# Attention and a SoLU feed-forward by two-level Strassen products: one operand made on GpSimd, and the last tile's steps moved to later slots

## The chip, the cores and the metric

The kernel runs on one NeuronCore of a Trainium2 chip. The metric is the device time of one launch in microseconds. Engines are named as in the profile: PE (TensorE; PEld is its weight load), DVE (VectorE), ACT (ScalarE), POOL (GpSimd), SP (the engine that issues most DMAs).

## The reference

```python
# q, k, v: (8, 12, 448, 64); g_q, g_k: (64,)
q_n, k_n = rmsnorm(q, g_q), rmsnorm(k, g_k)
attn = softmax(q_n @ k_n.T / sqrt(64))
x = (attn @ v).transpose(0, 2, 1, 3).reshape(3584, 768)
h = x @ w_in                              # w_in: 768 x 1024
e = exp(h - max(h)); solu = h * e / (sum(e) + 1e-9)
ln = (solu - mean(solu)) / sqrt(var(solu) + 1e-6) * g_ln
out = ln @ w_out                          # w_out: 1024 x 768
```

The change lies where the rows of `ln` are finished and the product with `w_out` begins.

## The kernel before

**Stages.** The first stage computes the attention and writes x to DRAM. The middle stage takes the 3584 rows as 28 tiles of 128 rows, in 14 groups g of two tiles (2g and 2g+1), and forms h = x w_in with Strassen's seven products (P1 to P7) per group. The last stage takes the normalized tiles four at a time, as 7 blocks n (block n has tiles 4n to 4n+3), and multiplies them by w_out with Strassen's scheme at two levels: seven outer products per block, each of seven inner products. The order of everything is written out by hand: each engine runs its instructions in the order in which the Python emits them, and the framework adds the semaphores.

**A tile's steps after its h is complete.** `ff_max` (DVE, tiny), `ff_exp` (ACT, L1067: u = exp(h - max)), `ff_mult` (DVE, L1071: u = h * u, which frees h), `ff_moments` (DVE: two batch-norm statistics L1079, their join L1080, three tiny instructions to L1084; then POOL: a power, L1085, called "pow" below, and "shift", L1087), `ff_norm` (ACT, L1091: u = u * e + shift), `ff_spread` (DVE: a transpose in blocks, L1100, from u to a buffer ub; then four stores on SP's queue, L1103, to the DRAM array ud of that tile). Multiplication, moments, scaling and spread in the title are `ff_mult`, `ff_moments`, `ff_norm` and `ff_spread`. Buffers h and u have three slots each and ub two, and the last stage's outputs use these same buffers in turn.

**When these steps are emitted.** `done(g, i)` is called inside products P4 (i = 1, tile 2g+1) and P3 (i = 0, tile 2g), the last two products of a group. It puts the five steps on a list with `later(x, f)`: due x units after the current one. A unit of the middle stage counts four steps, a slot of the last stage one. So for the last group (g = 13), a step of tile 27 given x is emitted in slot 4x - 9 of the last stage, a step of tile 26 (the tile that ends last) in slot 4x - 5; if that slot holds no product, in the next that does.

**Slots of the last stage.** One inner product is one slot: four matmul records of 128x192, KC = 2 chunks of two passes each. Outer product q (in the order P1, P5, P6, P2, P7, P3, P4 for each block; q counts on through the blocks) puts its seven inner products p1, p2, p6, p5, p7, p4, p3 into slots 7q + (0, 4, 8, 10, 12, 16, 20). So up to three outer products are interleaved, and from slot 14 on every slot is taken; slots 1, 2, 3, 5, 6, 9 and 13 are empty. Slot 20 is p3 of q = 0, slot 24 p5 of q = 2, slot 26 p7 of q = 2, slot 37 p4 of q = 3, slot 40 p7 of q = 4.

Three kinds of PSUM banks are used, A, B and C; B and C have two each (by q % 2), A four. p1 begins bank A and p6, p7, p4 go on adding to it, each after the one before has been read; p5 begins bank B and p3 adds to it; p2 uses C. What empties them:

- p1, p6, p7: the running sums q1, u2, u3 (L1222 on ACT for P1 and P5, else L1224 on DVE), and p4 likewise its result;
- p2: L1249 on DVE; p7 also reads bank B by L1262 on DVE; p3 by L1272 on DVE. So p5 of product q + 2 can begin only when L1272 of product q has read the same bank.

**Operands.** An outer product needs an operand of [128, 2, 4, 4, 32] (two token tiles, t = 0 and 1), made from the rows of ud that `load_u` brings back (L1147, SP) by `make(n, name, t)`, one instruction per t: a11, a12 and a22 are copies on ACT; s1, s2, s3, s4 are sums or differences on DVE (L1171, L1173, L1175, L1177). For block 0, a11 and s1 are made during the middle stage. From an operand `inner_sums` makes the four sums of the inner level with four POOL instructions of 128x256, L1188 to L1191, into one of four buffers. p1 and p2 (the halves of t = 0) and p4 (t = 1) use the operand itself, p6 the second of these sums, p5 the first, p7 the third, p3 the fourth.

`when(slot, f)` emits f at the end of a slot, after the product and after the steps due there. For block 0: s2 in slots 0 and 3, s3 in 6 and 8, a12 in 10 and 11, a22 in 12 and 14, s4 in 17 and 20; the sums of the operand of outer product q in slot 7q - 6, so those of s2 (q = 2) in slot 8, a12 15, s3 22, s4 29, a22 36. In slots 10 to 22 SP gets eight loads for block 1; in slots 18 and 21 ACT makes block 1's a11 and in slots 27 and 30 DVE its s1. V (L1300, DVE) is made in slots 31 and 34.

Of the kernel before, what the change touches and what calls it, by code (L numbers as in the profile page):

```python
# [14 lines left out]
OP = AluOpType  # L15
# [351 lines left out]
def fast_path(  # L367
# [24 lines left out]
    nc = tc.nc  # L392
# [11 lines left out]
    NG = NT // 2  # L404
# [535 lines left out]
    def load_x(g):  # L940
        x = gs[g, "x"] = xs.tile([P, KD, 2 * P], FP32, tag="x", name="xg")
        t = 2 * g * P
        while t < 2 * (g + 1) * P:
            b, c = divmod(t, S)
            n = min(S - c, 2 * (g + 1) * P - t)
            o = t - 2 * g * P

            (nc.sync if g < 2 else nc.scalar).dma_start(x[:, :, o : o + n], xd[b].rearrange("(c p) t -> p c t", p=P)[:, :, c : c + n])
            t += n

    def sizes(g):

        x = gs[g, "x"].rearrange("p c t -> p (c t)")
        n = HD * 2 * P
        sm = gs[g, "s"] = xs.tile([P, 3, HD, P], FP32, tag="x", name="xsum")
        for i in range(2):
            nc.scalar.activation(
                sm.rearrange("p k c t -> p (k c t)")[:, 0:n], x[:, i * n : (i + 1) * n], AF.Square,
                accum_out=xmax[:, 2 * g + i : 2 * g + i + 1],
            )  # L960
# [7 lines left out]
    def block_sums(g, part):  # L968

        if part == 0:  # L970
            gs[g, "A"] = x_blocks(g)
        a11, a12, a21, a22 = gs[g, "A"]
        sm = gs[g, "s"]
        s1, s2, s4 = [sm[:, i] for i in range(3)]
        if part == 0:
            nc.gpsimd.tensor_tensor(s1, a21, a22, OP.add)
            nc.gpsimd.tensor_tensor(s2, s1, a11, OP.subtract)
        else:
            nc.gpsimd.tensor_tensor(a21, a11, a21, OP.subtract)
            nc.gpsimd.tensor_tensor(s4, a12, s2, OP.subtract)  # L980
# [77 lines left out]
    def ff_max(t):  # L1058
        d = mt[t]
        d["nmax"] = small.tile([P, 1], FP32, tag="hmax", name="hmax")  # L1060
        nc.vector.tensor_scalar(d["nmax"], d["top"], -1.0, None, OP.mult)  # L1061
# [46 lines left out]
    def in_parts():  # L1108
        def done(g, i):
            t = 2 * g + i  # L1110
            ff_max(t)
            waits = {
                (NG - 2, 1): (1, 2, 3, 5, 5), (NG - 1, 1): (1, 2, 3.25, 6.75, 7), (NG - 1, 0): (2.25, 3.75, 4.75, 7.5, 8)
            }.get((g, i), (1, 2, 3, 5, 7))
            for x, f in zip(waits, (ff_exp, ff_mult, ff_moments, ff_norm, ff_spread)):
                later(x, lambda f=f: f(t))

        p = [products(g, lambda i, g=g: done(g, i)) for g in range(NG)]
        parts = [p[0][1], p[0][2]]
        for g in range(NG):  # L1120
            turn = [p[g][6], p[g][5], p[g][7], p[g][4], p[g][3]]
            x = len(parts)
            if g + 1 < NG:
                turn[3:] = [p[g + 1][1], p[g][4], p[g + 1][2], p[g][3]]
            parts += turn
            if g + 1 < NG:
                follow(parts, x, lambda g=g: sizes(g + 1))
                follow(parts, x + 1, lambda g=g: block_sums(g + 1, 0))
                follow(parts, x + 2, lambda g=g: block_sums(g + 1, 1))
            if g + 2 < NG:  # L1130
                follow(parts, x + 4, lambda g=g: load_x(g + 2))
        return parts

    ORDER = ("P1", "P5", "P6", "P2", "P7", "P3", "P4")
    STEP = 7
# [6 lines left out]
    us = {}  # L1142

    def load_u(n, t, h):
        own = last.get("u", last["first"])
        r = us[n, "raw", t, h] = own.tile([P, P * HF], FP32, tag="raw", name="ur", bufs=2 if own is last["first"] else 6)
        nc.sync.dma_start(r, ud[4 * n + t][h].rearrange("g j x -> (g j) x"))  # L1147

    def in_turn(n, t, h):
        return us[n, "raw", t, h].rearrange("p (a c i) -> p c a i", a=4, c=HF)  # L1150

    def operand(n, name):
        own = last.get("u", last["first"])
        if (n, name) not in us:
            us[n, name] = own.tile(
                [P, 2, HF, 4, 32], FP32, tag="op", name=name, bufs=2 if own is last["first"] else 8
            )
        return us[n, name]

    def make(n, name, t):  # L1160


        o = operand(n, name)[:, t]
        if name == "a11":
            nc.scalar.copy(o, in_turn(n, t, 0))
        elif name == "a12":
            nc.scalar.copy(o, in_turn(n, t, 1))
        elif name == "a22":
            nc.scalar.copy(o, in_turn(n, 2 + t, 1))
        elif name == "s1":  # L1170
            nc.vector.tensor_tensor(o, in_turn(n, 2 + t, 0), in_turn(n, 2 + t, 1), OP.add)  # L1171
        elif name == "s2":
            nc.vector.tensor_tensor(o, us[n, "s1"][:, t], us[n, "a11"][:, t], OP.subtract)  # L1173
        elif name == "s3":
            nc.vector.tensor_tensor(o, us[n, "a11"][:, t], in_turn(n, 2 + t, 0), OP.subtract)  # L1175
        else:
            nc.vector.tensor_tensor(o, us[n, "a12"][:, t], us[n, "s2"][:, t], OP.subtract)  # L1177

    def inner_sums(n, name):

        own = last.get("u", last["first"])
        a = us[n, name]
        sm = us[n, name, "sums"] = own.tile(
            [P, 4, KC, 4, 32], FP32, tag="sums", name="sums", bufs=2 if own is last["first"] else 4
        )
        a11, a12, a21, a22 = [a[:, t, k * KC : (k + 1) * KC] for t in range(2) for k in range(2)]
        s1, s2, s3, s4 = [sm[:, i] for i in range(4)]
        nc.gpsimd.tensor_tensor(s1, a21, a22, OP.add)  # L1188
        nc.gpsimd.tensor_tensor(s2, s1, a11, OP.subtract)
        nc.gpsimd.tensor_tensor(s3, a11, a21, OP.subtract)  # L1190
        nc.gpsimd.tensor_tensor(s4, a12, s2, OP.subtract)  # L1191
# [104 lines left out]
    def both(n, x, t):  # L1296

        if (n, x) not in us:
            us[n, x] = out_tile(x)
        nc.vector.tensor_tensor(us[n, x][:, t], us[n, "U2" if x == "V" else "U3"][:, t], us[n, "P5"][:, t], OP.add)  # L1300
        if x == "C22" and t == 0:
            store_y(n, us[n, x], 1, 1)

    def follow(p, i, f):
        g = p[i]

        def both():
            g()
            later(1, f)

        p[i] = both
# [7 lines left out]
    def later(units, f):  # L1319
        todo.append((now + 4 * units, f))  # L1320
# [49 lines left out]
    with tc.manual_schedule():  # L1370
# [228 lines left out]
        def when(slot, f):  # L1599
            at.setdefault(slot, []).append(f)  # L1600

        def made(n, name, *slots_of):
            for t, slot in enumerate(slots_of):
                when(slot, lambda t=t: make(n, name, t))

        period = STEP * len(ORDER)
        for n in range(NS):
            base = period * n
            for i, name in enumerate(ORDER):
                q = len(ORDER) * n + i  # L1610
                for place, f in zip(PLACES, outer_product(n, name, q)):
                    assert STEP * q + place not in slots
                    slots[STEP * q + place] = f
                x = HALVES[name][0]
                if q > 1:
                    when(STEP * q - 6, lambda n=n, x=x: inner_sums(n, x))
            for x, t, slot in (("V", 1, 31), ("V", 0, 34), ("C22", 1, 45), ("C22", 0, 52)):
                when(base + slot, lambda n=n, x=x, t=t: both(n, x, t))
            if n == 0:
                continue  # L1620
            base -= period
            at_load = (10, 11, 15, 16, 17, 18, 21, 22) if n == 1 else (4, 5, 8, 9, 10, 11, 16, 17)
            blocks = (0, 0), (1, 0), (2, 0), (3, 0), (2, 1), (3, 1), (0, 1), (1, 1)
            for slot, (t, h) in zip(at_load, blocks):
                when(base + slot, lambda n=n, t=t, h=h: load_u(n, t, h))
            late = 6 if n == 1 else 0
            made(n, "a11", base + 12 + late, base + 15 + late)
            made(n, "s1", base + 21 + late, base + 24 + late)
            made(n, "s2", base + 28 + late, base + 38)
            made(n, "a12", base + 33, base + 36)  # L1630
            made(n, "s3", base + 40, base + 42)
            made(n, "s4", base + 47, base + 49)
            made(n, "a22", base + 53, base + 55)
# [5 lines left out]
            load_u(0, t, 1)  # L1639
        for x in ("s2", "a12", "s3", "s4", "a22"):  # L1640
            operand(0, x)
        made(0, "s2", 0, 3)
        made(0, "s3", 6, 8)
        made(0, "a12", 10, 11)
        made(0, "a22", 12, 14)
# [87 lines left out]
```

## Time and profile before

| | us |
|---|---|
| median of 3 runs | 809.93 (808.85, 809.93, 811.12) |
| the profiled execution | 809.46 |
| its span, first to last instruction | 807.7 |
| PE busy | 793.2 (98%) |
| DVE busy | 615.4 (76%) |
| POOL busy | 505.7 (63%) |
| ACT busy | 474.0 (59%) |
| slot 0 of the last stage begins | 571.50 |
| slot 40 begins | 599.41 |

Times in the trace count from the start of the span. A timeline line gives start, duration, engine, line, operation, output <- inputs (128x512 is partitions x elements) and, in brackets, how long the engine was idle before and whose event ended that; a wait for several events is put down to the one that came last. Instructions of DVE overlap a little in the records: the next one starts some 0.08 us before the end of the one before, so that queue times are best added from start to start.

### The profile page before, as it was taken

The page shows a single profiled execution, that of the slowest core. Times are in us where ns is not written, and L with a number is a line of the kernel's source. Part 1 is how long each engine was busy: PE and PEld are TensorE (multiplying, and loading weights), DVE is VectorE, ACT ScalarE, POOL GpSimd, SP SyncE. Part 2 cuts the span into 40 slices and gives each one's busy share as a digit, 9 for nine tenths or more (in the row PEclk, how much of TensorE's full clock was granted, in tenths as well). Part 3 has the DMA queues.
Part 4 walks back from the last instruction along what each step waited for, and adds up shares of the span by engine and source line. Part 5 has one row for each costly group of instructions (what it writes and reads, how often), then busy time and mean ns, then how long its engine had stood idle before and what let it go on. Part 6 is the DMA issues. An engine that isn't in the chain of part 4 may idle for free.

```text
span 807.7 us, 14348 instructions
## 1 busy us (share of the span) xinstructions
PE 793.2 (98%) x4894; PEld 466.1 (58%) x4894; DVE 615.4 (76%) x1217; ACT 474.0 (59%) x785; POOL 505.7 (63%) x652
## 2 busy tenths in 40 slices
PE   8999999999999999999999999999899999999997
PEld 4334444444434444444444444444699999999996
DVE  6877889889888897488878667776886776866945
ACT  6677878778787774466766544453515455464420
POOL 1353677777777685234456466678487777777861
PEclk9999999999999999999999999999999999999999
DMA  9867798988877833545555445542647447365412
GB/s 164 176 149 150 166 191 191 190 180 175 172 155 165 155 97 97 139 122 153 153 135 138 110 108 144 140 116 52 209 119 256 144 176 267 117 227 192 141 60 83
DMA packets 269598, 122.68 MB, mean 152 GB/s; under 512 B 187596, under 2 KB 254668, under 8 KB 269516
## 3 DMA queue, kind: packets, MB, share of 16 engines
q1 hardware_dynamic: 254332, 111.78, 55.6%
q10 hardware_dynamic: 15184, 9.90, 4.5%
q8 instruction: 40, 0.66, 0.4%
q14 instruction: 42, 0.34, 0.1%
HBM read 84.94 MB, written 36.70 MB: 151 GB/s over the span
## 4 chain that ended last, share of the span: by engine, by line
PE 91%; DVE 4%; ACT 1%; DMA 1%; POOL 1%; issue 1%; SPq 0%; DVEq 0%; POOLq 0%; ACTq 0%
PE A L1210 15%; PE o L875 13%; PE s L818 13%; PE A L996 13%; PE B L996 8%; PE B L1210 7%; PE sm L897 5%; PE C L996 4%; PE D L996 4%; PE C L1210 4%; PE o L864 2%; PE s L831 2%; DMA ur<-ud 1%; ACT E L808 1%; DVE ub L1100 1%
## 5 line engine op out<-in xcount | busy, mean ns | idle before, releaser
L808 ACT ACTIVATE E<-s 128x896 f32<-128x896 f32 x168 | 139.1, 934 | 13.7 <-PE s L818 13.0
L818 PE MATMUL s<-qkT 64*64 64x448 f32 x1152 | 120.3, 545 | 1.4 <-ACT E L808 0.7
L875 PE MATMUL o<-E,v 128*64 128x448 f32 x576 | 113.5, 543 | 0.0
L1085 POOL TENSOR_TENSOR he<-he,mhalf 128x1 f32<-128x1 f32 x28 | 27.6, 987 | 105.4 <-DVE he L1084 104.9
L719 POOL TENSOR_TENSOR qkn<-qk,ny 128x896 f32<-128x896 f32 x46 | 77.2, 1698 | 21.1 <-DMA qk<-in_k_dram 15.1
L1210 PE MATMUL B<-w_out,sums 128*128 128x192 f32 x392 | 80.4, 328 | 2.8 <-DVE P L1272 2.1
L818 PEld LDWEIGHTS s<-qkT 64*64 64x64 f32 x1152 | 48.1, 163 | 59.3 <-ACT E L808 28.9
L1210 PE MATMUL A<-w_out,sums 128*128 128x192 f32 x392 | 80.7, 329 | 1.0 <-POOL sums L1191 0.7
L875 PEld LDWEIGHTS o<-E,v 128*64 128x64 f32 x576 | 39.2, 137 | 72.6 <-issue 67.3
L996 PE MATMUL B<-w_in,xsum 128*128 128x512 f32 x168 | 76.7, 593 | 0.4 <-POOL he L1085 0.4
L996 PE MATMUL A<-w_in,xg 128*128 128x512 f32 x168 | 74.6, 593 | 0.0
L1067 ACT ACTIVATE u<-h,hmax 128x1024 f32<-128x1024 f32 x28 | 32.1, 1148 | 62.9 <-DVE hmax L1061 62.8
L1210 PEld LDWEIGHTS B<-w_out,sums 128*128 128x128 f32 x392 | 66.8, 191 | 3.4 <-DVE P L1272 2.4
L1210 PEld LDWEIGHTS A<-w_out,sums 128*128 128x128 f32 x392 | 66.8, 191 | 1.7 <-POOL sums L1191 1.6
L680 POOL COPY ss<-part 32x56 f32<-32x56 f32 x88 | 42.0, 477 | 25.4 <-DVE part L670 21.0
L996 PEld LDWEIGHTS B<-w_in,xsum 128*128 128x128 f32 x168 | 31.8, 190 | 40.9 <-issue 38.5
L996 PEld LDWEIGHTS A<-w_in,xg 128*128 128x128 f32 x168 | 31.8, 190 | 40.1 <-issue 39.6
L854 POOL TENSOR_TENSOR es<-es,E 128x896 f32<-128x896 f32 x17 | 35.9, 2110 | 30.4 <-ACT sq L662 30.4
L845 DVE TENSOR_TENSOR es<-E 128x896 f32<-128x896 f32 x48 | 53.2, 1110 | 0.5 <-ACT E L808 0.5
L729 DVE STREAM_TRANSPOSE qkT<-qkn 128x896 f32<-128x896 f32 x46 | 48.5, 1089 | 1.8 <-POOL qkn L719 1.8
L670 DVE TENSOR_REDUCE part<-sq 128x28 f32<-128x896 f32 x46 | 48.2, 1078 | 2.2
L1210 PE MATMUL A<-w_out,s 128*128 128x192 f32 x224 | 45.6, 326 | 0.0
(152 smaller groups left out, 1658.0 us busy)
## 6 DMA issues: line engine op xcount, KB each, us to landing
ur<-ud SPq DMA_DIRECT2D x60, 256.0 KB, 4.9
ud<-ub SPq DMA_DIRECT2D x112, 128.0 KB, 2.3
xd<-xo SPq DMA_DIRECT2D x48, 224.0 KB, 3.0
qk<-in_q_dram SPq DMA_DIRECT2D x92, 112.0 KB, 3.1
qk<-in_k_dram SPq DMA_DIRECT2D x92, 112.0 KB, 3.0
v<-in_v_dram SPq DMA_DIRECT2D x24, 384.0 KB, 4.5
out_dram<-P SPq DMA_DIRECT2D x19, 384.0 KB, 4.0
raw<-in_moe_w_in_dram SPq DMA_DIRECT2D x12, 512.0 KB, 5.3
```

The costliest lines, as they stand in the source:

```text
L670: nc.vector.tensor_reduce(norms[m]["part"][:, i], st[n]["sq"], AX, OP.add)
L680: e.tensor_copy(ss[g * 32 : g * 32 + 32], part[o * 32 : o * 32 + 32])
L719: e.tensor_tensor(d["qkn"].rearrange("p (s b) d -> p s b d", s=2), d["qk"].rearrange("p s (b d) -> p s b d", d=32), y.rearrange("p (s b) - ...
L729: nc.vector.transpose(d["qkT"].rearrange("p s t -> p (s t)"), d["qkn"].rearrange("p b d -> p (b d)"))
L808: nc.scalar.activation(d["E", kc], s[:, :, 0:S], AF.Exp)
L818: nc.tensor.matmul(s[c : c + D, h, 0:S], d["qkT"][hh, 1, keys], d["qkT"][hh, 0, :], start=True, stop=True,)
L845: nc.vector.tensor_tensor(d["es"], d["E", 0], d["E", 1], OP.add)
L854: e.tensor_tensor(d["es"], d["es"], d["E", 2], OP.add)
L875: nc.tensor.matmul(d["o"][h * D : (h + 1) * D, :], quads[n // 2]["v"][:, n % 2 + 2 * h, kc], d["E", kc][:, h], start=False, stop=(kc == NJ ...
L897: nc.tensor.matmul(sm[g : g + 32, :], ones[:, w], e[:, h, t * S // 2 : (t + 1) * S // 2], start=(x == 0), stop=(x == len(terms) - 1),)
L996: nc.tensor.matmul(k[bank], a[:, c], w_in[i][:, c], start=begin and c == 0, stop=c == HD - 1, skip_group_check=not begin,)
L1210: nc.tensor.matmul(k[bank], a[:, c].rearrange("p a i -> p (a i)"), w_out[:, area, i, c], start=begin and c == 0, stop=c == KC - 1, skip_gr ...
```

## The change

The subtraction that makes s2 of block 0 goes from DVE to POOL, and its second half is emitted in slot 1 instead of 3; the inner sums of s2 of block 0 are emitted in slot 5 instead of 8. Later blocks keep theirs. For tile 26, the multiplication moves from slot 10 to 12, the moments from 14 to 22, the scaling from 25 to 27 and the spread from 27 to 30; for tile 27 the spread moves from slot 19 to 20.

```diff
@@ done(g, i) in in_parts
-                (NG - 2, 1): (1, 2, 3, 5, 5), (NG - 1, 1): (1, 2, 3.25, 6.75, 7), (NG - 1, 0): (2.25, 3.75, 4.75, 7.5, 8)
+                (NG - 2, 1): (1, 2, 3, 5, 5), (NG - 1, 1): (1, 2, 3.25, 6.75, 7.25), (NG - 1, 0): (2.25, 4.25, 6.75, 8, 8.75)
@@ make(n, name, t)
         elif name == "s2":
-            nc.vector.tensor_tensor(o, us[n, "s1"][:, t], us[n, "a11"][:, t], OP.subtract)
+            (nc.vector if n else nc.gpsimd).tensor_tensor(o, us[n, "s1"][:, t], us[n, "a11"][:, t], OP.subtract)
@@ the last stage's plan
                 if q > 1:
-                    when(STEP * q - 6, lambda n=n, x=x: inner_sums(n, x))
+                    when(STEP * q - 6 if q > 2 else 5, lambda n=n, x=x: inner_sums(n, x))
@@ block 0's operands
-        made(0, "s2", 0, 3)
+        made(0, "s2", 0, 1)
```

## The prediction

> **What bounds the kernel now.** The page's first table has PE busy for 98% of the span, so only idle or slow PE time can be won. The waits of PE say where it lies: between 600 and 801 us PE waits 0.4 us in all; the change's stretch is the start of the last stage. Busy time by windows (columns: stretch, its length, then busy us and count of PE, PEld, DVE, ACT, POOL, granted clock, DMA):
>
> ```profile
> 571.40:580.40 9.00, 8.80 (x53) 8.29 (x51) 8.50 (x17) 5.11 (x13) 1.81 (x2) 1.00 0.65 188
> 580.40:586.90 6.50, 3.67 (x22) 3.20 (x21) 6.33 (x16) 4.04 (x6) 6.08 (x10) 1.00 0.65 224
> 586.90:590.40 3.50, 3.50 (x13) 3.50 (x12) 1.57 (x6) 0.00 (x0) 3.42 (x5) 0.51 0.93 236
> 590.40:600.00 9.60, 8.94 (x55) 8.52 (x54) 9.32 (x19) 1.24 (x2) 7.68 (x10) 1.00 0.30 80
> 600.00:801.00 201.00, 200.63 (x1235) 200.17 (x1235) 141.96 (x343) 86.54 (x192) 142.70 (x168) 1.00 0.50 168
> ```
>
> DVE is full up to 586.9 and again from 590.4; PE is half empty in the second row, and in the third it works at half clock. After 600 PE is full. The timeline names the pieces:
>
> ```profile
> 568.82 0.27 POOL L1087 TENSOR_SCALAR shift<-mv,he 128x1 f32<-128x1 f32 x1
> ...
> 573.70 1.29 DVE L1173 TENSOR_TENSOR s<-s,a 128x512 f32<-128x512 f32 x2
> ...
> 578.49 0.86 POOL L1085 TENSOR_TENSOR he<-he,mhalf 128x1 f32<-128x1 f32 x1 [9.40 <-DVE he L1084]
> ...
> 579.46 1.22 DVE L1071 TENSOR_TENSOR u<-h,u 128x1024 f32<-128x1024 f32 x1
> 580.86 0.35 DVE L1262 TENSOR_TENSOR P<-B,u 128x192 f32<-128x192 f32 x1
> 581.27 0.92 PE L1210 MATMUL B<-w_out,sums 128*128 128x192 f32 x4 [0.69 <-DVE P L1262]
> ...
> 584.75 1.23 DVE L1100 STREAM_TRANSPOSE ub<-u 128x1024 f32<-128x1024 f32 x1
> 585.91 0.31 DVE L1272 TENSOR_TENSOR P<-B,u 128x192 f32<-128x192 f32 x1
> 586.28 1.02 PE L1210 MATMUL B<-w_out,sums 128*128 128x192 f32 x4 [2.14 <-DVE P L1272]
> 587.09 1.49 PE L1210 MATMUL C<-w_out,a 128*128 128x192 f32 x4
> ...
> 588.62 0.36 DVE L1249 TENSOR_TENSOR P<-C,q 128x192 f32<-128x192 f32 x1 [0.97 <-PE C L1210]
> ...
> 598.93 0.34 DVE L1224 TENSOR_TENSOR u<-A,P 128x192 f32<-128x192 f32 x1
> ...
> 599.41 0.89 PE L1210 MATMUL A<-w_out,sums 128*128 128x192 f32 x4 [0.66 <-POOL sums L1191]
> ```
>
> PE starts a slot every 0.65 us and waits for DVE to empty a bank: 0.69 us before slot 20 (586.28 is slot 24, 599.41 slot 40), 2.14 us before slot 24, then runs half as fast, so that DVE itself waits 0.97, 0.92 and 0.21 us (**2.10 us**), and waits once more at slot 40. The last row names POOL, but the sums POOL finishes then are a22's, which slot 40 does not read; what it needs is the bank that L1224 at 598.93 reads. So slot 40 is set by DVE's queue, and all after it follows at PE's pace: the end moves as slot 40 moves.
>
> **What the Trainium skill says.** "TensorE: Matmul & The Clock Gate", Part 1, has half clock after an idle window of about 3.4 us. Here the trace's clock was half for 3.41 us (586.97 to 590.38) after one wait of 2.14 us; waits of 0.69 left it full. So a wait well under 3.4 us can do it, and where the step lies between 0.69 and 2.14 no row shows. "GPSIMD Engine Reference", section 3, prices a two-input `tensor_tensor` at about twice DVE's; section 1 says that it contends with DVE instructions that have two SBUF inputs. The trace agrees: 0.73 us for 256 elements and 1.00 for 384 uncontended, against DVE's 0.68 for 512; contended ones of 256 took 1.17.
>
> **The change part by part.**
>
> *s2 to GpSimd.* Two DVE instructions go (573.70 to 574.90 with the next one's start: **1.20 us**). POOL gets two of 128x512; by 0.73 and 1.00 (0.27 for 128 elements) about 1.3 us each, as L563's 512 at 1.35. Inputs are long there, and POOL is idle from 569.1 to 578.5, so they run from 569.1 to about 571.7, or, should their memory only come free with the previous stage's last multiplication (571.7), to about 574.5 under the contention of L1071. PE needs the first at slot 14, 576.05: cost nothing; without that idle POOL, up to 2.6 us.
>
> *Sums of s2 from slot 8 to slot 5.* On POOL they stay behind he and shift of tile 27, so they only follow these forward. Slot 22 needs the second of them: ready about 581.3, slot due 581.7. Nothing.
>
> *DVE from 573.70, in start-to-start times of this trace.* L1249 0.27, spread of tile 24 1.16, moments of 27 1.93, two s3 1.20, L1249 and L1262 0.53: L1262 starts 578.5 instead of 580.86, and slot 20 goes at 580.41 with no wait. Then L1071 of tile 26 (moved here, slot 12) 1.14, L1224 0.27, s4 0.60, L1249 0.27: 581.1. Here L1262 of slot 19 waits for ACT's u3, which is queued behind the chain pow 0.86 and shift 1.36 (POOL), norm 1.24 and a11 0.6 (ACT) of tile 27: u3 ends about 581.7. **New idle 0.58 us.** Pow and shift at their shortest (0.55, 0.27) remove it; at their longest (1.46, 1.36) it is 1.2. L1262 and then L1272 (now ahead of the spread) end by 582.3; slot 24 is due at 583.01. The 2.14 us wait is gone, and with it the cause of half clock.
>
> *Spread of 27, slot 19 to 20.* 1.16, then s4 0.88 and L1224 0.27: L1224's u starts at 584.5, ends 584.85. Slot 26 wants it at 584.31: **new wait 0.6 us**, the price of the spread now standing ahead of these. What is behind the spread otherwise: its four stores on SP, then two loads for block 1, still earlier than before (585.98), since spread ends 583.5.
>
> *Moments of 26, slot 14 to 22; norm 25 to 27; spread 27 to 30.* DVE work between L1224's u of slot 22 and that of slot 36 (587.30 and 598.93) was 11.63 us with 2.10 idle: 9.53 of work, the spread of 26 among it. Moments add 2.2 (581.39 to 583.62). So u of slot 36 starts at 584.5 + 9.53 + 2.22 = 596.25, and slot 40 at 596.25 + 0.48 = **596.7**, against 599.41. On POOL, pow and shift of 26 now stand ahead of the sums of s3, at about 587.5 to 588.7; sums follow to 591.6, slot 36 needs theirs near 592. ACT has nothing between slots 23 and 33 but this norm, 588.7 to 590.0; the spread comes up on DVE at 590.2: covered with 0.2 us to spare. The spread's four stores on SP land by about 597; the first to need that buffer is C22, slot 45, near 600. Block 6, which reads tiles 26 and 27, is over 100 us away. Cover gone: see the second rival.
>
> Sum: 1.20 + 2.10 - 0.58 = **2.7 us** sooner at slot 40. PE's new waits lie inside DVE's time and are not added: from slot 26 at 584.9, 11 slots of 0.65 bring it to slot 37 at 592.1, whose bank L1224's u3 of slot 33 (595.77 before, 3.16 ahead of the 598.93) frees only at 593.5, 1.4 late; three slots on, slot 40 is due at 595.5 and 1.2 late. The profiled execution took 809.46 us, its span 807.7; 2.7 less is 806.8 and 805.0. It lies 0.47 under the median of 809.93, so the forecast of the median is **807.2**.
>
> **Rivals.**
>
> *Half clock all the same, or not in all runs of before* (0.23). Slots 37 and 40 wait 1.4 and 1.2 us with 1.95 of work between, so a window of 3.41 us holds at most some 1.5 of it; one window at half clock loses PE 3.41 / 2 = 1.7 us, hidden no longer once DVE has caught up: 2.7 - 1.7 = 1.0 sooner, 808.9. The other form: in a run of before without half clock, DVE's 2.10 idle would shrink by some 1.3, leaving a gain of 1.4: 808.5. For it: the step is unknown above 0.69, and the three times shown differ by 2.3 us. Against: 1.5 stays below the 2.14 that did it.
>
> *Tile 26's chain makes DVE wait at slot 30* (0.12; slower). Margin 0.2 us. If POOL's eight sums of s2 and a12 take 1.17 each as contended ones did (9.4 from 579.7: 589.1 instead of 586.0), pow 1.46, shift 1.36 and norm 1.24 end near 593.3, and the spread, with V and everything behind it, is held 3.1 us. That wait empties PE long enough for half clock, of one window or of two (1.7 or 3.4): -2.7 + 3.1 + 1.7 = 2.1 slower, or 3.8; between them 3.0, 812.9. It decides where shift ends over 2.9 us late (2.7 and the margin), or 1.2 with one window of half clock. Against: only single instructions were stretched so far, never eight in a row.
>
> *The change does nothing:* had slot 40 waited for POOL, as the view says, and not for DVE, a22's sums would set it; these wait for slot 34 and so follow PE. Included in the first rival.
>
> **Numbers.** Main case 0.65: 2.7, bounded by the idle of 0 to 1.2 at slot 19 (+0.6, -0.6) and by contention of POOL with DVE's two-input instructions elsewhere, which can go either way by some 0.4, what one such sum lost (1.17 for 0.73): 1.6 to 3.8, 806.1 to 808.3. 0.3% is 2.43 us, about what a measurement of this kernel can tell from no change. Faster 0.56 (the larger part of the main case), same 0.33 (its lower end, the first rival, a little of the second), slower 0.11. The range, 805.9 to 809.4, holds the main case and the first rival and leaves out the slower one.
>
> **What would show it.** Right: L1173 twice on POOL before 574; no PE wait at slots 20 and 24; clock full from 571 to 600; DVE without a gap but near 581; the slot 40 multiplication at about 596.7 and its wait still for L1224. Wrong: a half-clock stretch near 590 to 598, the spread of 26 waiting for ACT, s2 on POOL late for slot 14, or PE waits after 600 that were not there.

## The result and the profile after

| | before | after |
|---|---|---|
| median, first comparison (6 runs each) | 809.68 | 806.74 |
| ratio of the runs, with 95% interval | | 0.9963 (0.995 to 0.9975) |
| the same in a second comparison (26 and 8 runs) | 809.46 | 806.99; 0.9971 (0.996 to 0.9982) |
| profiled execution, and its span | 809.46, 807.7 | 807.55, 805.7 |
| slot 0 in the profile | 571.50 | 572.78 |
| slot 40, counted from slot 0 | 27.9 | 24.8 |

The kernel became 2.5 to 2.9 us faster, by the medians of the two comparisons. The profile gained 3.1 us between slot 0 and slot 40; 1.3 of it were lost before slot 0. They were lost already when s2 begins on POOL (the shift ahead of it starts at 570.10 instead of 568.82), where nothing is changed. So times below are counted from slot 0 where kernels are compared.

The windows of the changed kernel (columns as before):

```profile
571.40:580.40 9.00, 9.00 (x51) 8.19 (x50) 7.21 (x17) 7.00 (x16) 3.17 (x5) 1.00 0.75 229
580.40:586.90 6.50, 5.89 (x37) 5.63 (x36) 6.50 (x12) 2.45 (x5) 6.34 (x8) 1.00 0.84 278
586.90:590.40 3.50, 3.50 (x24) 3.49 (x22) 3.36 (x13) 1.73 (x3) 2.77 (x5) 1.00 0.70 222
590.40:600.00 9.60, 7.63 (x45) 6.91 (x44) 9.50 (x19) 0.59 (x2) 9.44 (x12) 1.00 0.25 57
600.00:799.00 199.00, 198.63 (x1223) 198.05 (x1222) 140.51 (x339) 86.52 (x192) 141.26 (x167) 1.00 0.50 169
```

In the third row PE now has 24 matmul records where it had 13, at full clock. What PE still lacks stands in the second and the fourth row (5.89 of 6.50 and 7.63 of 9.60). DVE is full in the second, third and fourth; in the first it waits 1.91 us for the middle stage's last product, as before. The timeline shows the pieces:

```profile
570.32 2.51 POOL L1173 TENSOR_TENSOR s<-s,a 128x512 f32<-128x512 f32 x2
...
579.53 0.26 POOL L1087 TENSOR_SCALAR shift<-mv,he 128x1 f32<-128x1 f32 x1
...
580.08 1.49 DVE L1071 TENSOR_TENSOR u<-h,u 128x1024 f32<-128x1024 f32 x1
...
580.56 1.59 POOL L1189 TENSOR_TENSOR sums<-sums,s 128x256 f32<-128x256 f32 x1
...
581.75 0.94 DVE L1177 TENSOR_TENSOR s<-a,s 128x512 f32<-128x512 f32 x1
582.62 0.34 DVE L1249 TENSOR_TENSOR P<-C,q 128x192 f32<-128x192 f32 x1
582.89 0.34 DVE L1262 TENSOR_TENSOR P<-B,u 128x192 f32<-128x192 f32 x1
583.15 0.34 DVE L1272 TENSOR_TENSOR P<-B,u 128x192 f32<-128x192 f32 x1
583.42 1.23 DVE L1100 STREAM_TRANSPOSE ub<-u 128x1024 f32<-128x1024 f32 x1
...
585.90 0.89 PE L1210 MATMUL A<-w_out,sums 128*128 128x192 f32 x4 [0.61 <-POOL sums L1189]
...
593.99 0.92 PE L1210 MATMUL A<-w_out,a 128*128 128x192 f32 x4 [0.60 <-DVE u L1224]
...
597.10 0.34 DVE L1224 TENSOR_TENSOR u<-A,P 128x192 f32<-128x192 f32 x1
...
597.59 0.89 PE L1210 MATMUL A<-w_out,sums 128*128 128x192 f32 x4 [1.37 <-POOL sums L1189]
```

s2 runs on POOL up to slot 0 of the last stage (572.78), 2.51 us for both halves. DVE goes from L1249 through L1262 to L1272 without a gap, and L1272 starts 10.4 us after slot 0 instead of 14.4. PE waits at slots 26 (585.90), 37 (593.99) and 40 (597.59), and no longer at 20 and 24. The first and third of these name POOL's L1189, but the sums that it makes there are a12's and a22's, which slots 26 and 40 do not read. Experiment e8 tests this for slot 40; for slot 26 it is read from the operands and from L1224, which ends just before it, and no run tests it.

### The profile page after: what moved, and what is told of

It is laid out like the page before. It is cut to its first block, busy times and chain, and to the rows that moved or that the text cites. A ratio compares the mean times of both kernels' runs of the same rounds, so it can differ in the third digit from the quotient of the medians.

```text
span 805.7 us, 14347 instructions
## 1 busy us (share of the span) xinstructions
PE 792.0 (98%) x4894; PEld 464.2 (58%) x4894; DVE 615.6 (76%) x1215; ACT 473.7 (59%) x785; POOL 507.2 (63%) x654
## 4 chain that ended last, share of the span: by engine, by line
PE 87%; DVE 5%; ACT 2%; POOL 2%; issue 1%; DMA 1%; SPq 0%; DVEq 0%; ACTq 0%
PE A L1210 14%; PE A L996 13%; PE o L875 12%; PE s L818 12%; PE B L996 8%; PE B L1210 7%; PE C L996 4%; PE sm L897 4%; PE D L996 4%; PE C L1210 3%; PE o L864 2%; PE s L831 2%; ACT E L808 1%; PE pt L772 1%; DMA xg<-xd 1%
## 5 line engine op out<-in xcount | busy, mean ns | idle before, releaser
L680 POOL COPY ss<-part 32x56 f32<-32x56 f32 x88 | 41.8, 475 | 25.5 <-DVE part L670 21.0
```

The source lines that it names most:

```text
L680: e.tensor_copy(ss[g * 32 : g * 32 + 32], part[o * 32 : o * 32 + 32])
```

## The experiments

Start of the slots in each profile, in us from slot 0, and the comparison with the kernel before:

| kernel | slot 24 | slot 33 | slot 40 | ratio (95%) |
|---|---|---|---|---|
| before | 14.8 | 22.5 | 27.9 | |
| b2: before again | 14.8 | 22.5 | 27.9 | |
| after | 11.1 | 17.8 | 24.8 | 0.9963 (0.995 to 0.9975) |
| a2: after again | 11.1 | 17.8 | 24.8 | 0.9971 (0.996 to 0.9982) |
| e1: s2 only | 13.6 | 19.8 | 25.6 | 0.9985 (0.9978 to 0.9992) |
| e2: slots only | 12.0 | 19.0 | 26.1 | 0.9996 (0.9988 to 1.0004) |
| e3: before and filler | 14.8 | 21.0 | 26.8 | 1.0002 (0.9994 to 1.0011) |
| e4: sums in slot 8 | 11.1 | 17.8 | 24.8 | 0.9976 (0.9965 to 0.9987) |
| e5: s3 on POOL too | 11.1 | 17.6 | 24.6 | 0.9969 (0.9958 to 0.9981) |
| e8: block 1 later | 11.1 | 17.8 | 22.3 | 0.9942 (0.9928 to 0.9956) |
| e9: spread back in 27 | 11.1 | 20.0 | 26.3 | 0.9985 (0.9976 to 0.9993) |
| e10: before, block 1 later | 14.8 | 20.9 | 25.5 | 0.9993 (0.9982 to 1.0004) |

**e1, the operand alone.**

```diff
-            nc.vector.tensor_tensor(o, us[n, "s1"][:, t], us[n, "a11"][:, t], OP.subtract)
+            (nc.vector if n else nc.gpsimd).tensor_tensor(o, us[n, "s1"][:, t], us[n, "a11"][:, t], OP.subtract)
-                    when(STEP * q - 6, lambda n=n, x=x: inner_sums(n, x))
+                    when(STEP * q - 6 if q > 2 else 5, lambda n=n, x=x: inner_sums(n, x))
-        made(0, "s2", 0, 3)
+        made(0, "s2", 0, 1)
```

> Only s2 of block 0 goes to GpSimd (slots 0 and 1, its sums in slot 5); the last tiles' steps stay where they were. Theory A (two terms: 1.2 us of DVE work gone, and half clock gone because the order of the tile steps changed): DVE's queue before L1272 of slot 20 still holds the moments of tile 26 and the spread of 27, so PE waits about 1.5 to 2.5 us before slot 24, half clock stays, and the gain is about 1.2 us (0.15%). Theory B (the shorter DVE queue alone removes the slow stretch; the slots are incidental): no half clock near 587, no wait over 1 us before slot 24, and the gain is 2.5 to 3 us (0.3 to 0.4%).

Measured: 0.15% faster (1.2 us), as theory A had it; B, which expected no wait over 1 us and 2.5 to 3 us, is out. But A had one thing wrong. The timeline of e1 around slot 24:

```profile
582.95 0.81 PE L1210 MATMUL A<-w_out,s 128*128 128x192 f32 x4
585.91 0.92 PE L1210 MATMUL B<-w_out,sums 128*128 128x192 f32 x4 [2.14 <-DVE P L1272]
586.66 0.81 PE L1210 MATMUL C<-w_out,a 128*128 128x192 f32 x4
```

The wait is the 2.14 us of before, to the hundredth, and yet the multiplication behind it takes 0.81 and not 1.49: full clock. So the wait does not decide it. The granted clock in the traces changes only at multiples of 3.413 us from its last change (580.266 us is 170 of them before, 798.72 is 234 in e1). Before, the wait from 584.14 to 586.28 lies wholly in the window that ends at 586.97. In e1, counting back from the clock's change at 803.42, a window ends at 584.97, and splits the wait (583.77 to 585.91) into 1.20 and 0.94 us. Experiment e10 meets the same wait split in another place.

**e2, the slots alone.**

```diff
-... (NG - 1, 1): (1, 2, 3.25, 6.75, 7), (NG - 1, 0): (2.25, 3.75, 4.75, 7.5, 8)
+... (NG - 1, 1): (1, 2, 3.25, 6.75, 7.25), (NG - 1, 0): (2.25, 4.25, 6.75, 8, 8.75)
```

> Only the slots of the last two tiles' steps change; s2 stays on DVE. Theory A: the wait before slot 24 falls to about 1 us or is spread over slots 22, 24 and 26 (0.8 and 1.0), the clock stays full, DVE's 2.1 us of idle go, and the gain is 1.3 to 2 us (0.16 to 0.25%). Theory B: without the shorter queue the wait only moves to another slot, half clock comes all the same, and the gain is under 0.5 us.

Measured: 0.04% faster, not told from nothing; the interval ends at 0.12%, or 1.0 us, so A's 1.3 to 2 is missed. What A said of the trace holds in this profile: the clock is full, the waits before slots 22 and 26 are 0.42 and 0.78 us (none is left before slot 24), and DVE has no idle left. A had put all of the 2.1 us of idle on each run of before. Counted in slot 40 from a profile of full clock (e3 below, 26.8), e1 brings 1.2 us, e2 0.8 and the whole change 2.0: the two parts add up.

**How often half clock strikes.** The list of runs gives each one's mean granted clock. A window of half clock lowers it by 0.002 (3.41 / 2 of 807 us), so 0.997 or less is an approximate mark of it. It is approximate because each profile also ends at half clock, after PE's last multiplication, for 0.8 to 4.1 us of its span, and because it does not say where in the span the window lay. In the twelve profiles it agrees with the stretch looked at here: the three with a half-clock window there (before, b2, e9) have the mark, the other nine don't. In the three later comparisons 43 of 82 runs of before have that mark. Their mean is 810.0 us; that of the other 39 is 808.9. So half clock costs about 1.1 us where it strikes, and strikes in about half of the runs. Of e1's 18 runs 6 have the mark, of e2's 13 it is 4: by this mark, neither part alone removes it. Of the 14 runs of the changed kernel 2 have the mark; the mean of the other 12 is 806.8. Without half clock, then, the change brings about 2.0 us.

**b2, the kernel before, once more.**

> The kernel before once more, for a second profile. If half clock struck only by the phase of a window of 3.41 us against the 2.14 us wait, this profile shows the same wait before slot 24, and may show a full clock; slot 40 then lies 26.5 to 27.0 us after slot 0 instead of 27.9.

Its profile has half clock again, with 2.11 of the same 2.14 us inside a window that ends at 586.18 (multiplication behind it from 586.21, 1.65 us). A profile of before at full clock is therefore not there. Two that have slot 24 tied to L1272 as before, the same DVE order behind it and full clock stand in for it: e1, with the same wait, and e3, where a filler takes up most of the wait. DVE is idle 0.71 and 0.72 us there, against 2.10 and 2.18 in the two profiles of before.

**e3, a filler in the wait.**

```diff
+        def filler():
+            x = us[0, "a12"]
+            spare = last["ps"].tile([P, 512], FP32, tag="C1", name="spare")[:, 0:N2]
+            for _ in range(3):
+                for c in range(KC):
+                    nc.tensor.matmul(spare, x[:, 0, KC + c].rearrange("p a i -> p (a i)"), w_out[:, 1, 1, c], start=c == 0, stop=c == KC - 1)
+        when(23, filler)
```

> The kernel before, with six extra multiplications of 128x192 (three times the product of slot 25, into its own bank, which that slot then begins anew) after slot 23, where PE waited 2.14 us. They take 3 x 0.65 = 1.95 us and compute nothing that is used. Theory A (half clock by itself costs, since it makes DVE idle): clock full from 571 to 600, slot 24 no later than before, and 1.3 to 2.1 us faster (0.16 to 0.26%). Theory C (half clock costs nothing, as DVE is the bound there anyway): within 0.3 us, or slower by what of the filler sticks out.

Its windows:

```profile
580.50:587.00 6.50, 5.45 (x32) 5.16 (x33) 6.33 (x16) 4.04 (x6) 6.08 (x10) 1.00 0.66 223
587.00:590.50 3.50, 3.50 (x22) 3.29 (x21) 2.75 (x8) 0.00 (x0) 3.42 (x5) 1.00 0.89 210
```

Slot 24 is where it was (14.8), the clock is full, DVE works 2.75 instead of 1.57 us in the second row, and slot 40 is 1.1 us sooner than in the profile of before. The mark of half clock is on 1 of 13 runs instead of one in two. But the median didn't move, so A's gain of 1.3 to 2.1 us is missed, and by the time alone C would be right. The list of runs gives each one's span beside its time, and shows where the gain went. In the 41 runs of before in this comparison the time is 1.75 to 1.85 us longer than the span; with the filler it is 1.8 to 2.9 us longer (median 2.4), as in no other kernel here. The spans themselves average 807.0 against 807.5 for before, which fits 1.1 us gained in half of the runs. Why time is added outside the span is not shown, and stays open.

**e4, the sums in slot 8 again.**

```diff
-                    when(STEP * q - 6 if q > 2 else 5, lambda n=n, x=x: inner_sums(n, x))
+                    when(STEP * q - 6, lambda n=n, x=x: inner_sums(n, x))
```

> The changed kernel with the inner sums of s2 again in slot 8. POOL's order is pow and shift of tile 27, then these sums, then a12's, in both cases. Theory A: no difference from the changed kernel, 0.37% faster than before. If the earlier sums mattered, slot 22 would now wait on POOL.

Same slots as a2 to 0.01 us and an interval that covers a2's ratio: this part of the change does nothing. The gain, 0.24%, is less than the 0.37% expected from the first comparison; the interval ends at 0.35%. POOL runs the sums behind pow and shift of tile 27 either way.

**a2, the changed kernel again.**

> The changed kernel once more, beside the variants below on one chip. From the first comparison: 0.25 to 0.5% faster than before. If part of that came from half clock, which struck only in some of the runs of before, the gain should shrink where those are left out: about 2.0 us among runs of full clock against about 2.5 among all.

0.29% (2.5 us by the medians). Among the runs of this comparison without the mark the gain is 1.9 us, near the 2.0 expected.

**e5, one more operand to POOL.**

```diff
-            nc.vector.tensor_tensor(o, us[n, "a11"][:, t], in_turn(n, 2 + t, 0), OP.subtract)
+            (nc.vector if n else nc.gpsimd).tensor_tensor(o, us[n, "a11"][:, t], in_turn(n, 2 + t, 0), OP.subtract)
-        made(0, "s3", 6, 8)
+        made(0, "s3", 2, 3)
```

> The changed kernel with block 0's s3 on GpSimd too, in slots 2 and 3 (POOL is idle there), which takes 1.2 us from DVE's queue just as the move of s2 did. Theory A (slot 40 follows DVE's total work): 1.2 us faster than the changed kernel. Theory D (work taken from DVE ahead of slot 19 pays no more, since DVE there meets ACT's u3, which waits for a11's load): 0 to 0.3 us faster, with DVE idle some 0.8 us before L1262 of slot 19.

0.31% against the 0.29% of a2: no gain. The timeline shows the idle that theory D expected:

```profile
580.81 0.34 DVE L1249 TENSOR_TENSOR P<-C,q 128x192 f32<-128x192 f32 x1
581.76 0.36 DVE L1262 TENSOR_TENSOR P<-B,u 128x192 f32<-128x192 f32 x1 [0.60 <-ACT u L1222]
```

DVE gets to L1262 of slot 19 sooner and stands there for 0.60 us. ACT's u3 comes behind norm of tile 27, which waited 0.78 us for POOL's shift, and behind one a11 (D had named a11's load, for which nothing waits here). Another 0.3 us goes to the first L1071, which takes 1.45 us from start to start beside POOL's s3, against 1.13 in the changed kernel. Slot 40 is 0.2 sooner. A move of 1.2 us that paid in full with s2 paid a fifth of it with s3.

**e9, the spread of tile 26 back in slot 27.**

```diff
-... (NG - 1, 0): (2.25, 4.25, 6.75, 8, 8.75)
+... (NG - 1, 0): (2.25, 4.25, 6.75, 8, 8)
```

> The changed kernel with the spread of tile 26 in slot 27 again, everything else as changed. Moments of that tile end on DVE near 587.6, its norm on ACT near 589.9. Theory A: DVE stands before the spread from about 588.8 to 589.9, and all behind it (L1224's u of slot 29 for slot 33) is late by about 1.1 us: 1.0 to 1.5 us slower than the changed kernel. Theory F (the spread's slot doesn't matter, as PE waits later anyhow): no difference.

The timeline:

```profile
587.90 0.35 DVE L1272 TENSOR_TENSOR P<-B,u 128x192 f32<-128x192 f32 x1
...
589.36 1.25 DVE L1100 STREAM_TRANSPOSE ub<-u 128x1024 f32<-128x1024 f32 x1 [1.11 <-ACT u L1091]
...
591.65 0.34 DVE L1224 TENSOR_TENSOR u<-A,P 128x192 f32<-128x192 f32 x1
...
592.14 0.89 PE L1210 MATMUL A<-w_out,sums 128*128 128x192 f32 x4 [2.05 <-POOL sums L1188]
...
592.87 1.44 PE L1210 MATMUL B<-w_out,sums 128*128 128x192 f32 x4
```

DVE stands 1.11 us before the spread, for norm on ACT; slot 33 (592.14) is 2.2 us later than in the changed kernel. The view names POOL's sums for its wait, but these are s4's, while slot 33 reads a12's third sum, done at 585.90; what it needs is the bank that L1224 at 591.65 reads. DVE's stand makes up 1.1 of the 2.2 us; the rest is that this L1224 now comes behind the spread. The wait of 2.05 us, in one window again (its end is at 592.91), brings half clock back. The median, 808.08, is 1.1 us above the changed kernel's 806.99, as expected. 9 of its 16 runs have the mark. Moments in slot 22 and spread in slot 30 belong together.

**e8, block 1's operands later, on top of the change.**

```diff
-            made(n, "s1", base + 21 + late, base + 24 + late)
-            made(n, "s2", base + 28 + late, base + 38)
+            if n == 1:
+                made(n, "s1", base + 41, base + 43)
+                made(n, "s2", base + 46, base + 48)
+            else:
+                made(n, "s1", base + 21, base + 24)
+                made(n, "s2", base + 28, base + 38)
-            made(n, "s3", base + 40, base + 42)
-            made(n, "s4", base + 47, base + 49)
+            made(n, "s3", *((base + 50, base + 52) if n == 1 else (base + 40, base + 42)))
+            made(n, "s4", *((base + 54, base + 56) if n == 1 else (base + 47, base + 49)))
```

> The changed kernel with block 1's s1, s2, s3, s4 made in slots 41 to 56 instead of 27 to 49, so that DVE's queue before the u2 of slot 36 loses two s1 (1.04 and 0.57 from start to start) and one s2 (1.13). Theory A (the remaining waits of PE, 0.61, 0.60 and 1.37 us, are DVE's queue): these waits mostly go, 1.5 to 2.5 us faster than the changed kernel. Theory E (slot 40 waits for POOL's sums, as the view names): the wait before slot 40 stays, nothing gained.

Slot 40 is at 22.3, 2.5 us sooner than in the changed kernel. The waits of PE in all of 571.7 to 600:

```profile
PE A L1210 <- POOL sums L1189: 0.6, 1, 0.6
```

That is slot 26 alone; those of slots 37 and 40 are gone, although POOL's list of sums was not touched. The order in time around slot 40 settles which engine it waited for:

```profile
593.11 0.35 DVE L1224 TENSOR_TENSOR u<-A,P 128x192 f32<-128x192 f32 x1
...
594.07 0.81 PE L1210 MATMUL A<-w_out,sums 128*128 128x192 f32 x4
...
594.76 0.73 POOL L1189 TENSOR_TENSOR sums<-sums,a 128x256 f32<-128x256 f32 x1
```

Slot 40 begins before the sum that the view had named in the changed kernel has even begun. The wait put down to POOL was DVE's. Median 804.78 against 806.99 for the changed kernel and 809.46 for before: this version beats both, by 2.2 and 4.7 us. Not all of slot 40's 2.5 us is kept: from slot 0 to PE's last multiplication 1.7 us are left, since PE now waits 0.64 us for L1272 at 607.24, where the changed kernel doesn't wait.

**e10, the same edit on the kernel before.**

> The kernel before with block 1's s1 to s4 in slots 41 to 56, and nothing of the change. Theory A: the wait before slot 24 stays at 2.1 us, since what moves is emitted after it; the waits after slot 28 go; 0.5 to 1.5 us faster than before, well short of what the same edit gave on top of the change (2.2).

0.07% (0.6 us; 0.1 by the medians), its interval reaching past nothing; the wait of 2.14 us is there as before:

```profile
586.43 0.92 PE L1210 MATMUL B<-w_out,sums 128*128 128x192 f32 x4 [2.14 <-DVE P L1272]
587.18 0.81 PE L1210 MATMUL C<-w_out,a 128*128 128x192 f32 x4
```

Behind it the clock is full, as in e1. Counting back from the clock's change at 803.25, a window ends at 584.80 and splits this wait (584.29 to 586.43) into 0.51 and 1.63 us; so 1.63 us of waiting in one window was not enough for half clock.

Slot 40 comes 2.5 us sooner than in the profile of before, but with full clock, and 1.4 sooner than in e3; half of the 1.4 is lost again in a wait of 0.68 us for L1272 at 610.29. The edit is worth more behind the change, though the interval here doesn't say how many times more. In the kernel before, PE's wait before slot 24 lets DVE catch up, and less is left behind it to win: from slot 24 to slot 40 PE falls 1.7 us behind its pace in e3, but 3.4 us in the changed kernel.

## Why the prediction was right, point by point

- **What bounds.** DVE's queue from 573 to 600, read from the windows and from the waits at slots 20, 24 and 40. e8 confirms the reading of slot 40 against the view, which names POOL in before and in after.
- **s2 to GpSimd.** Expected at about 1.3 us each, from before slot 0 on and hidden; measured 2.51 for both, done at slot 0. Worth 1.20 us; alone it measured 1.2 (e1), and slot 40 is 1.2 us sooner in e1 than in e3.
- **Sums sooner.** Nothing, and nothing was measured (e4).
- **New idle of 0.58 us at slot 19.** Wrong in its form. Shift took 0.26 and not 1.36 us (its shortest, which the step had as the one end), and no idle was left. Instead DVE and POOL slowed each other: from start to start L1071 took 1.41 for 1.14 and the first s4 0.87 for 0.60, while POOL's sum took 1.59 for 0.73. The second s4 took 0.57 for 0.88. The net of these is 0.23.
- **Waits of PE.** 0.6 us at slot 26, 1.4 at slot 37 and 1.2 at slot 40 were forecast. The records have 0.61, 0.60 and 1.37; against the pace of 0.65 it is 0.77, 0.76 and 1.54. Slot 37's was put too high. That the waits lie inside DVE's time and don't add holds.
- **Tile 26's chain.** Norm ended at 589.91, the spread began at 590.59 with no wait. Seven tenths of margin instead of 0.2; e9 shows what the second rival would have looked like, at 1.1 us and with half clock.
- **The 2.10 us of DVE's idle.** This term of the sum was mis-sized. It stands in the profile of before, and in that profile the whole gain from slot 0 to slot 40 is 3.1 us, against 2.7 predicted. But about half of the runs of before have full clock, and there only some 0.7 us of idle are to be won (e1, e3). 1.20 + 0.7 - 0.23 makes 1.7, and the runs without the mark differ by 2.0. The missing 0.3 is again the contention of POOL and DVE: where the kernel before runs at full clock (e3), L1171 and V take 0.4 us more than in the profile of before (the first L1300 1.00 us from start to start, not 0.47), and for the same reason half clock costs 1.1 us and not the 1.4 of its idle. The first rival's second form had this right, and nearly its size: it put the idle that half clock adds at 1.3 us (2.10 less 0.71 is 1.4), and the gain then left at 1.4, where 2.0 was measured. Both cases are true at once, each in about half of the runs.
- **The total.** 807.2 predicted, 806.74 and 806.99 measured. Slot 40 was put at 596.7; it came at 597.59, which is 596.3 if slot 0 is set back to its place in before. The path was right: DVE's queue, shortened by s2 and by the wait that went. That the number fits so closely is in part luck: the mis-sized term and the contention were made up for by the idle that did not come.

## What to carry to other kernels

Where PE waits for one engine's queue over a long stretch, add up that queue's work from the first wait to the last: what is removed pays in full only if no other engine's result is waited for in between (s2 paid 1.2 us, s3 0.2). A step that is delayed must be delayed with all that hangs on it, or its wait lands in the queue it was meant to clear (e9). Before an idle or a slow clock in one profile is counted as gain, look in the list of runs for how many have it. Where a view names a late event for a wait, check that the waiting instruction reads what that event made (e8).

## What the runs showed of the hardware

- The granted clock is decided over fixed windows of 3.41 us, as the Trainium skill has it ("TensorE: Matmul & The Clock Gate", Part 1: a window of 3413 ns that doesn't start anew with the kernel). But the window need not be idle, though the page's table of states asks for an idle one: 2.05 us (e9) and 2.11 to 2.14 us of waiting inside one (before, b2) were enough for half clock in the next. The same 2.14 us across a boundary was not, split into 1.20 and 0.94 (e1) or into 0.51 and 1.63 (e10), nor was a wait of 1.37 us (after). So the step lies between 1.63 and 2.05 us of waiting in one window of 3.41, as far as these profiles show.
- GpSimd and DVE can slow each other when both run instructions with two inputs in SBUF (on DVE L1071, L1171 to L1177 and L1300): an inner sum of 256 elements took 1.59 us beside L1071 and L1177, against 0.73 alone or beside the transposes and the moments (583.25 and 585.77 in after). GpSimd's 512-element subtraction, alone, took 1.25 us (half of the 2.51) against DVE's 0.68; the skill's page "GPSIMD Engine Reference", section 3, says about twice.
